# From group 6 on, one DMA transposes q and k of both groups of a block, and one DMA transposes x of both

## The chip, the cores and the metric

The kernel runs on one core of a Trainium2 chip. Its metric is the device time of one execution in microseconds (us). The engines carry the names of the profile: PE (TensorE, matmul), PEld (its weight load), DVE (VectorE), ACT (ScalarE), POOL (GpSimd) and SP (SyncE, which here only issues DMAs). All of SP's DMAs go into one queue, q1, and the stores that POOL issues go into q0.

## The reference

Attention inside chunks of 64 tokens, then a feed-forward layer with a squared ReLU. Cut to what matters:

```python
# q, k, v: (8 batches, 8 heads, 576 tokens, 64)
scores = scale * np.matmul(q_c, k_c.transpose(0, 1, 2, 4, 3))   # per chunk of 64 tokens
scores = scores - np.max(scores, axis=-1, keepdims=True)
attn = np.exp(scores)
attn = attn / (np.sum(attn, axis=-1, keepdims=True) + 1e-09)
out = np.matmul(attn, v_c)
x = out.transpose(0, 2, 1, 3).reshape(B * S, H * D)             # (4608, 512)
h = np.maximum(x @ w_in, 0.0)                                   # w_in (512, 2048)
return (h * h @ w_out).astype(np.float32)                       # w_out (2048, 512)
```

## The kernel before

**Tiling.** The 4608 tokens are cut into 18 groups of 256 tokens (four chunks), and two groups make a block of 512. There are nine blocks, j = 0 to 8. Block j holds groups 2j and 2j+1. Groups 14 and 15 are put together from the leftover chunks of four batches each, so their loads are more and smaller.

**Software pipeline.** While PE works on the feed-forward of block j, the attention of block j+1 (`nxt`) is worked between its matmuls, and the inputs of block j+2 (`far`) are loaded, cast and transposed. The order is written out by hand. A block is a row of slots: for j from 2 on, slots 0 to 15 are the 16 tiles of `ffn_in` (four matmuls of 128x512 each), and slots 16 to 29 are the 14 half products of `ffn_out` (eight matmuls of 128x256 each). In block 1, `ffn_in` is in two halves and has slots 0 to 31. After each slot the loop at L663 to L673 first issues one load, if the slot is among `go_slots`, and then the steps that the plan has there.

The steps that the change touches are these, in the order in which a group goes through them:

- `C`, `cast_qk` (L252): two casts, q and k from float32 to bfloat16, into the tile `qkb`. They run on POOL for groups under 8 and on ACT from group 8 on.
- `TD`, `transpose_qk_dma` (L263): one DMA transpose on SP from `qkb` to `qkT`, 128x2048 bfloat16 (512 KB) for a group. It is used from group 4 on.
- `SC`, `scores` (L271): 32 small matmuls from `qkT`, and the exponential on ACT into the tile `e`.
- `AV`, `values` (L303): matmuls of `e` with v, and the division on DVE into the tile `x` (L325).
- `XT`, `transpose_x` (L331): from group 6 on, one DMA transpose on SP from `x` to half of the block's `xT`, 128x1024 bfloat16 (256 KB) for a group. `ffn_in` of that block reads `xT` (L380).

SP[...] takes its instructions in program order: a transpose that waits for its source holds back every load that is written behind it. The plan for j from 3 on (L644):

```python
slots = {SC: (6, 6), AV: (9, 13), XT: (12, 16), C: (18, 22), TD: (20, 24)}
```

The pair of numbers is for the first and the second group. `SC` is at (8, 10) in block 2, at (8, 8) in block 3, at (7, 7) in block 4 and at (5, 5) where the next groups are whole. In block 1 the far groups 6 and 7 have `C` at 36 and 40 and `TD` at 42 and 45 (L635).

Between `C` and `TD` of the two groups lie ACT's other duties in `ffn_out`: the copies n1 (L492, after slot 17) and n2 (L501, after slot 21), which take a product out of PSUM before PE may add the next product of the same chain.

Of the kernel before, what the change touches and what calls it, by code (L numbers as in the profile page):

```python
# [11 lines left out]
BF16 = mybir.dt.bfloat16  # L12
# [5 lines left out]
def kernel(  # L18
# [9 lines left out]
    nc = tc.nc  # L28

    B, H, S, D = q.shape  # L30
# [4 lines left out]
    n_hp = H // 2  # L35
# [26 lines left out]
    att_pool = ctx.enter_context(tc.tile_pool(name="att", bufs=3))  # L62
# [123 lines left out]
    xTs = {}  # L186
# [4 lines left out]
    state = {}  # L191

    def transpose_paired(g, which, psb):

        src = qk[g][which].bitcast(BF16).rearrange(
            "p t h d -> p (t h d)").rearrange("p (h i d) -> p h i d", h=H, i=2)
        dst = psb.rearrange("c (h i q) -> c h i q", h=n_hp, i=2)
        for hp in range(n_hp):
            for i in range(2):
                for a in range(2):  # L200
                    nc.tensor.transpose(  # L201
                        out=dst[64 * a:64 * a + 64, hp, i, :],
                        in_=src[:, 2 * hp + a, i, 1::2],
                        identity=ident)
# [6 lines left out]

    def transpose_qk(g, q_pool, k_pool):
        if ("qkT", g) not in state:
            state["qkT", g] = att_pool.tile(
                [128, 2, 2, n_hp, 128], BF16, name="qkT", bufs=4)
        qkT = state["qkT", g]
        for which, pool in enumerate((q_pool, k_pool)):
            if pool is None:
                continue
            copy = nc.scalar.copy if which else nc.vector.tensor_copy  # L220
            if pool is ps_ffn:
                bank = pool.tile([128, 512], FP32, name="ps_ffn")
            else:
                bank = pool.tile([128, 1024], FP32, name="ps_att")
            bank = bank.bitcast(BF16)[:, 0:1024]
            transpose_paired(g, which, bank)
            copy_paired(copy, qkT[:, which], bank)
# [22 lines left out]
                rhs=ident[:, None, :].to_broadcast([128, m, 128]), start=True, stop=True)  # L250

    def cast_qk(g):  # L252
        qkb = att_pool.tile([128, 2, 2 * H * D], BF16, name="qkb", bufs=2)
        state["qkb", g] = qkb

        copy = nc.gpsimd.tensor_copy if g < 8 else nc.scalar.copy
        q_sb, k_sb = (x.rearrange("p t h d -> p (t h d)") for x in qk[g])
        copy(
            out=qkb[:, 0].rearrange("p (i h d) -> p i h d", i=2, h=H),
            in_=q_sb.rearrange("p (h i d) -> p i h d", h=H, i=2))  # L260
        copy(out=qkb[:, 1], in_=k_sb)  # L261

    def transpose_qk_dma(g):  # L263
        qkb = state.pop(("qkb", g))
        qkT = att_pool.tile([128, 2, 2, n_hp, 128], BF16, name="qkT", bufs=4)
        state["qkT", g] = qkT
        nc.sync.dma_start_transpose(
            out=qkT.rearrange("c w t h q -> c (w t h) q"),
            in_=qkb.rearrange("p w c -> p (w c)"))

    def scores(g):  # L271
        qkT = state.pop(("qkT", g))
        by_plane = g >= FIRST_DMA_T

        def queries(a, t, hp, p):
            x = qkT[64 * a:64 * a + 64, 0]
            if by_plane:
                p0 = (2 * t + p) * CH // 2
                return x[:, :, hp, p0:p0 + CH // 2]
            return x[:, t, hp, p * 64:p * 64 + 64]  # L280

        ps = ps_att.tile([128, 1024], FP32, name="ps_att")
        for hp in range(n_hp):
            for t in range(2):
                for a in range(2):
                    for p in range(2):
                        c = p ^ a
                        cols = slice(p * 64, p * 64 + 64)
                        o0 = a * 512 + hp * 128 + t * 64
                        nc.tensor.matmul(  # L290
                            out=ps[64 * c:64 * c + 64, o0:o0 + 64],
                            lhsT=qkT[64 * a:64 * a + 64, 1, t, hp, cols],
                            rhs=queries(a, t, hp, p),
                            start=True, stop=True)
        e = att_pool.tile([128, 2, n_hp, 2, 64], BF16, name="e")
        state["e", g] = e
        e_out, s_in = e.rearrange("p a h t q -> p (a h t q)"), ps
        if by_plane:
            e_out = e.rearrange("p a h t (q i) -> p (a h t) q i", i=2)
            s_in = ps.rearrange("p (b i q) -> p b q i", i=2, q=CH // 2)  # L300
        nc.scalar.activation(out=e_out, in_=s_in, func=AF.Exp, scale=scale)  # L301

    def values(g, tiles=(0, 1)):  # L303
        e = state["e", g]
        veb = v_even[g % NV].bitcast(BF16)
        vob = [v_odd[odd_tile[g, c] % NO].bitcast(BF16) for c in range(4)]
        if 0 in tiles:
            state["x", g] = att_pool.tile([128, 2, n_hp, 2, D], BF16, name="x", bufs=3)
        x = state["x", g]
        for t in tiles:  # L310
            ps = ps_att.tile([128, 2, 512], FP32, name="ps_att")
            for hp in range(n_hp):
                for a in range(2):
                    for p in range(2):
                        c = p ^ a
                        vb = vob[2 * t + p] if a else veb[:, t]
                        nc.tensor.matmul(  # L317
                            out=ps[64 * p:64 * p + 64, a, hp * (D + 1):(hp + 1) * (D + 1)],
                            lhsT=e[64 * c:64 * c + 64, a, hp, t, :],
                            rhs=vb[64 * c:64 * c + 64, hp, 1::2],  # L320
                            start=True, stop=True)
            o = ps[:, :, 0:n_hp * (D + 1)].rearrange("p a (h d) -> p a h d", d=D + 1)
            rec = att_pool.tile([128, 2, n_hp], FP32, name="rec", bufs=4)
            nc.vector.reciprocal(out=rec, in_=o[:, :, :, D])  # L324
            nc.vector.tensor_tensor(  # L325
                out=x[:, t].rearrange("p h a d -> p a h d"),
                in0=o[:, :, :, 0:D],
                in1=rec.to_broadcast([128, 2, n_hp, D]),
                op=ALU.mult)

    def transpose_x(g):  # L331
        j, c = place[g]
        if j not in xTs:
            xTs[j] = att_pool.tile([128, BT // 128, n_dt, 128], BF16, name="xT", bufs=2)
        x = state.pop(("x", g))
        dst = xTs[j][:, c // 128:c // 128 + 2].rearrange("p t h q -> p (t h) q")
        if g >= FIRST_DMA_X:
            nc.sync.dma_start_transpose(out=dst, in_=x.rearrange("p t h a d -> p (t h a d)"))
            return
        ps = ps_att.tile([128, 1024], FP32, name="ps_att")  # L340
        psb = ps.bitcast(BF16)[:, 0:1024].rearrange("p (b q) -> p b q", q=128)
        for t in range(2):
            for hp in range(n_hp):
                nc.tensor.transpose(
                    out=psb[:, t * n_hp + hp, :],
                    in_=x[:, t, hp].rearrange("p a d -> p (a d)"),
                    identity=ident)
        copy = nc.vector.tensor_copy if g == blocks[1][0] else nc.scalar.copy
        copy(out=dst, in_=psb)  # L349

    C, TD = cast_qk, transpose_qk_dma
    SC, AV, XT = scores, values, transpose_x

    def TA(g):
        transpose_qk(g, ps_att, ps_att)
# [254 lines left out]
    for j, grps in enumerate(blocks):  # L610
        nxt = blocks[j + 1] if j + 1 < len(blocks) else []
        far = blocks[j + 2] if j + 2 < len(blocks) else []
        plan = {}

        def at(slot, f, g):
            plan.setdefault(slot, []).append((f, g))
# [9 lines left out]
        elif j == 1:  # L626
# [7 lines left out]
                    at(slot, f, g)  # L634
            for i, g in enumerate(far):  # L635
                at(36 + 4 * i, C, g)
                at(42 + 3 * i, TD, g)
            at(2, sum_quarters(b11_p_b12, b11, b12), None)
            at(12, sum_quarters(b12_p_b22, b12, b22), None)
            at(20, sum_quarters(b21_p_b22, b21, b22), None)  # L640
            phases = [ffn_in(1, [(0, 256, FT_ORDER), (256, 256, FT_ORDER)]), ffn_out(1)]
        else:
            loads, go_slots = pieces(far), range(32)
            slots = {SC: (6, 6), AV: (9, 13), XT: (12, 16), C: (18, 22), TD: (20, 24)}  # L644
            if j == 3:
                slots.update({SC: (8, 8), AV: (10, 14), XT: (13, 17)})
                go_slots = [*range(6), *range(13, 32)]
# [3 lines left out]
                slots.update({SC: (5, 5), AV: (8, 12), XT: (11, 15)})  # L651
            if j == 2:
                loads = itertools.chain(*map(v_pieces, nxt), loads)
                slots = {SC: (8, 10), AV: (12, 15), XT: (15, 18), C: (20, 23), TD: (22, 25)}
                go_slots = [*range(16), 23, 24, *range(26, 36)]
            for f in (SC, AV, XT):
                for i, g in enumerate(nxt):
                    at(slots[f][i], f, g)
            for f in (C, TD):
                for i, g in enumerate(far):  # L660
                    at(slots[f][i], f, g)
            phases = [ffn_in(j, [(0, BT, FT_ORDER)]), ffn_out(j)]
        slot = 0  # L663
        for phase in phases:
# [40 lines left out]
```

## Time and profile before

| | us |
|---|---|
| median of 4 runs | 285.84 (283.2 to 290.56) |
| the profiled execution | 284.9 |
| its span on the core | 283.1 |
| around the span | 1.8 |
| PE at work at a clock of 1.00, blocks 2 to 6, each | 28.0 to 28.2 of 28.1 to 28.4 |

For each block from group 6 on, the transposes of q and k as the trace has them. An issue is the start of SP's instruction. A landing is that time plus the time to landing which the trace gives for it. "First scores" is the start of PE's score matmuls of the pair, which need these landings.

| groups | issued in block | first TD issued | second TD issued | first landed | second landed | first scores | second scores |
|---|---|---|---|---|---|---|---|
| 6, 7 | 1 | 79.4 | 84.2 | 86.3 | 92.1 | 90.90 | 93.11 |
| 8, 9 | 2 | 106.7 | 111.7 | 113.5 | 117.8 | 119.05 | 119.4 |
| 10, 11 | 3 | 136.2 | 140.7 | 142.8 | 146.4 | 146.30 | 146.7 |
| 12, 13 | 4 | 162.2 | 164.0 | 166.2 | 172.4 | 172.69 | 173.0 |
| 14, 15 | 5 | 189.1 | 194.1 | 194.7 | 200.8 | 201.63 | 202.0 |
| 16, 17 | 6 | 219.8 | 221.8 | 226.5 | 230.6 | 229.16 | 230.69 |

Where the scores of a pair run as one stretch of 64 matmuls in 0.71 us, the start of the second group is its middle. Such a table is read row by row: the column of the second landing against the two columns of the scores says how much time is left.

### The profile page before, as it was taken

The numbers are of one execution on the slowest core, as the hardware profiler recorded it, in microseconds if no ns is written. First come the engines' busy times: TensorE is split into PE (matmuls) and PEld (weight loads), VectorE is DVE, ScalarE is ACT, GpSimd is POOL, SyncE is SP. The second block draws the span as 40 slices with busy tenths as digits, with TensorE's granted clock in tenths as the row PEclk, the third lists the DMA queues.
The fourth block names the chain that finished last, engine by engine and source line by source line (L and its number), as shares of the span: only waits on it lengthen the run. The fifth ranks groups of instructions, "written<-read, shape, count | busy, mean of one in ns | idle before, by whom it ended". The sixth has DMA issues, their size and how long they took to land.

```text
span 283.1 us, 7169 instructions
## 1 busy us (share of the span) xinstructions
PE 270.1 (95%) x2954; PEld 175.4 (62%) x2954; DVE 185.8 (66%) x303; ACT 163.2 (58%) x277; POOL 55.7 (20%) x92
## 2 busy tenths in 40 slices
PE   1999999999999999999999999999999989999994
PEld 1554444778774487458745874587457734874583
DVE  1255514899943495579558953995399538955792
ACT  1458705786348862876287629762876286218710
POOL 2037843240161004000400040004000400060012
PEclk9999999999999999999999999999999999999999
DMA  7999999999998999998999899479799952142003
GB/s 201 242 325 362 360 340 237 299 218 219 202 238 239 226 212 211 280 251 167 241 256 221 180 258 252 100 160 213 209 244 185 191 150 39 37 105 46 1 28 123
DMA packets 140817, 57.10 MB, mean 202 GB/s; under 512 B 110640, under 2 KB 137520, under 8 KB 140784
## 3 DMA queue, kind: packets, MB, share of 16 engines
q1 hardware_dynamic: 137744, 47.33, 75.1%
q0 software_dynamic: 2896, 9.18, 9.6%
q8 instruction: 23, 0.38, 0.6%
q10 hardware_dynamic: 144, 0.13, 0.1%
q14 instruction: 10, 0.08, 0.1%
HBM read 36.70 MB, written 9.44 MB: 163 GB/s over the span
## 4 chain that ended last, share of the span: by engine, by line
PE 68%; DVE 15%; DMA 7%; ACT 5%; issue 3%; SPq 1%; ACTq 0%; DVEq 0%
PE ps_ffn L380 29%; PE ps_ffn L448 27%; DVE x L325 5%; DVE gT L395 5%; PE ps_ffn L538 5%; DMA k_sb<-in_k_dram 4%; DMA qkT<-qkb 3%; DVE w_st L408 3%; ACT rl L391 3%; PE ps_ffn L248 1%; ACT e L301 1%; PE ps_ffn L201 1%; PE ps_att L290 1%; DVE rec L324 1%; PE ps_att L317 1%
## 5 line engine op out<-in xcount | busy, mean ns | idle before, releaser
L380 PE MATMUL ps_ffn<-xT,w_in_bf 128*128 128x512 bf16 (+1 forms) x648 | 130.1, 356 | 0.2 <-DVE xT L349 0.2
L395 DVE TENSOR_TENSOR gT<-rl 128x512 bf16<-128x512 f32 (+2 forms) x130 | 74.0, 599 | 64.4 <-ACT rl L391 63.0
L391 ACT ACTIVATE rl<-ps_ffn 128x512 f32<-128x512 f32 (+2 forms) x162 | 86.0, 548 | 24.5 <-PE ps_ffn L380 21.9
L380 PEld LDWEIGHTS <-w_in_bf 128*128 128x128 bf16 x648 | 61.3, 98 | 56.6 <-DVE xT L349 0.4
L448 PEld LDWEIGHTS <-w_st 128*128 128x128 bf16 x640 | 61.7, 98 | 9.0 <-DVE w_st L408 1.8
L408 DVE TENSOR_TENSOR w_st<-gT 128x2048 bf16<-128x2048 bf16 x40 | 47.4, 1220 | 0.2
L448 PE MATMUL ps_ffn<-w_out_bf,w_st 128*128 128x256 bf16 x384 | 45.1, 273 | 0.4
L476 POOL DMA_DIRECT2D out_dram<-o_sb x25 | 17.8, 714 | 126.8 <-DVE o_sb L408 122.2
L448 PE MATMUL ps_ffn<-w_sum,w_st 128*128 128x256 bf16 x256 | 29.6, 273 | 0.0
L448 PEld LDWEIGHTS <-gT 128*128 128x128 bf16 x256 | 24.6, 98 | 5.0 <-DVE gT L395 0.8
L325 DVE TENSOR_TENSOR x<-ps_att,rec 128x512 bf16<-128x512 f32 x36 | 24.9, 692 | 1.2
L528 ACT COPY o_sb<-ps_ffn 128x512 f32<-128x512 f32 (+1 forms) x8 | 4.5, 560 | 35.4 <-PE ps_ffn L448 35.4
L301 ACT ACTIVATE e<-ps_att 128x1024 bf16<-128x1024 f32 x18 | 17.9, 1020 | 6.4 <-PE ps_att L290 6.4
L393 ACT ACTIVATE gT<-rl 128x512 bf16<-128x512 f32 (+2 forms) x32 | 18.4, 576 | 1.0
L448 PE MATMUL ps_ffn<-w_out_bf,gT 128*128 128x256 bf16 x128 | 15.6, 273 | 0.2 <-DVE gT L395 0.2
L448 PE MATMUL ps_ffn<-w_sum,gT 128*128 128x256 bf16 x128 | 15.3, 273 | 0.0
L538 PE MATMUL ps_ffn<-w_out_bf,gT 128*128 128x512 bf16 x64 | 14.5, 380 | 0.0
L169 POOL CAST w_in_bf<-w_st 128x512 bf16<-128x512 f32 (+2 forms) x12 | 9.9, 840 | 18.3 <-DMA w_st<-in_moe_w_in_dram 18.3
L501 ACT COPY n<-ps_ffn 128x512 f32<-128x512 f32 (+1 forms) x9 | 4.8, 538 | 12.3 <-PE ps_ffn L448 12.3
L317 PEld LDWEIGHTS <-e 64*64 64x64 bf16 x576 | 6.5, 107 | 7.4 <-issue 2.2
L261 ACT CAST qkb<-k_sb 128x1024 bf16<-128x1024 f32 x10 | 10.5, 1047 | 0.1
L290 PEld LDWEIGHTS <-qkT 64*64 64x64 bf16 x576 | 6.1, 110 | 7.2 <-issue 3.4
(53 smaller groups left out, 162.3 us busy)
## 6 DMA issues: line engine op xcount, KB each, us to landing
q_sb<-in_q_dram SPq DMA_DIRECT2D x16, 512.0 KB, 6.2
out_dram<-o_sb POOLq DMA_DIRECT2D x29, 256.0 KB, 4.6
k_sb<-in_k_dram SPq DMA_DIRECT2D x24, 256.0 KB, 5.9
ve_sb<-in_v_dram SPq DMA_DIRECT2D x32, 128.0 KB, 4.1
w_st<-in_moe_w_in_dram SPq DMA_DIRECT2D x8, 512.0 KB, 6.6
w_st<-in_moe_w_out_dram SPq DMA_DIRECT2D x8, 512.0 KB, 5.9
vo_sb<-in_v_dram SPq DMA_DIRECT2D x24, 128.0 KB, 3.7
k_sb<-in_k_dram SPq DMA_DIRECT2D x4, 512.0 KB, 7.1
```

The source lines that it names most:

```text
L169: copy(out=dst, in_=st[:, rows].rearrange("p a (f t) -> p a t f", t=2)[:, :, t])
L261: copy(out=qkb[:, 1], in_=k_sb)
L301: nc.scalar.activation(out=e_out, in_=s_in, func=AF.Exp, scale=scale)
L325: nc.vector.tensor_tensor(out=x[:, t].rearrange("p h a d -> p a h d"), in0=o[:, :, :, 0:D], in1=rec.to_broadcast([128, 2, n_hp, D]), op=AL ...
L380: nc.tensor.matmul(out=h[:, 0:n], lhsT=w_in_bf[:, dt, ft * 128:(ft + 1) * 128], rhs=xT[:, c // 128:(c + n) // 128, dt, :], start=(dt == 0) ...
L391: nc.scalar.activation(out=rl[:, 0:n], in_=h[:, 0:n], func=AF.Relu)
L393: nc.scalar.activation(out=gT[:, ft, c:c + n], in_=rl[:, 0:n], func=AF.Square)
L395: nc.vector.tensor_tensor(out=gT[:, ft, c:c + n], in0=rl[:, 0:n], in1=rl[:, 0:n], op=ALU.mult)
L408: engine.tensor_tensor(out=out, in0=in0, in1=in1, op=op)
L448: nc.tensor.matmul(out=outs[t], lhsT=a[:, i, t * 128:(t + 1) * 128], rhs=b[:, i, :], start=(first and i == 0 and (last or t == 0)), stop=( ...
L476: dma.dma_start(out=out[t0:t0 + HT, col:col + HD].rearrange("(t p) d -> p t d", p=128), in_=o_sb.rearrange("p (t d) -> p t d", d=HD))
L538: nc.tensor.matmul(out=o_ps[tt], lhsT=gT[:, ft, tt * 128:(tt + 1) * 128], rhs=w_out_bf[:, ft, :], start=(ft == 0), stop=(ft == n_ft - 1))
```

## The change

It has five parts.

1. `qkb` becomes one tile for both groups of a block with one buffer (before: one group, two buffers). `qkT` becomes a tile for both groups with two buffers (before: one group, four buffers). The bytes are the same.
2. From group 6 on the two `TD` become one, `TDB`, 1 MB, at slot 44 of block 1 (before 42 and 45), slot 24 of block 2 (before 22 and 25) and slot 22 of the later blocks (before 20 and 24).
3. `C` of the second group goes from slot 22 to 20 (in block 2 from 23 to 22).
4. `x` becomes a tile for both groups with two buffers (before: one group, three buffers), and `XT` issues nothing for the first group and one transpose of 512 KB for both at the second group's slot.
5. `e` has two buffers in place of three.

```diff
     def cast_qk(g):
-        qkb = att_pool.tile([128, 2, 2 * H * D], BF16, name="qkb", bufs=2)
-        state["qkb", g] = qkb
+        if g % 2 == 0:
+            state["qkb", g // 2] = att_pool.tile(
+                [128, 2, 2, 2 * H * D], BF16, name="qkb", bufs=1)
+        qkb = state["qkb", g // 2][:, g % 2]
...
+    def qkT_of(g):
+        if g % 2 == 0:
+            state["qkT", "block", g // 2] = att_pool.tile(
+                [128, 2, 2, 2, n_hp, 128], BF16, name="qkT", bufs=2)
+        return state["qkT", "block", g // 2][:, g % 2]
...
+    def transpose_qk_dma_block(g):
+
+        for i in range(2):
+            state["qkT", g + i] = qkT_of(g + i)
+        nc.sync.dma_start_transpose(
+            out=state["qkT", "block", g // 2].rearrange("c g w t h q -> c (g w t h) q"),
+            in_=state["qkb", g // 2].rearrange("p g w c -> p (g w c)"))
...
-        e = att_pool.tile([128, 2, n_hp, 2, 64], BF16, name="e")
+        e = att_pool.tile([128, 2, n_hp, 2, 64], BF16, name="e", bufs=2)
...
-            state["x", g] = att_pool.tile([128, 2, n_hp, 2, D], BF16, name="x", bufs=3)
+            if g % 2 == 0:
+                state["x", "block", g // 2] = att_pool.tile(
+                    [128, 2, 2, n_hp, 2, D], BF16, name="x", bufs=2)
+            state["x", g] = state["x", "block", g // 2][:, g % 2]
...
         if g >= FIRST_DMA_X:
-            nc.sync.dma_start_transpose(out=dst, in_=x.rearrange("p t h a d -> p (t h a d)"))
+
+            if g % 2:
+                nc.sync.dma_start_transpose(
+                    out=xTs[j].rearrange("p t h q -> p (t h) q"),
+                    in_=state["x", "block", g // 2].rearrange("p g t h a d -> p (g t h a d)"))
             return
...
                 at(36 + 4 * i, C, g)
-                at(42 + 3 * i, TD, g)
+            at(44, TDB, far[0])
...
-            slots = {SC: (6, 6), AV: (9, 13), XT: (12, 16), C: (18, 22), TD: (20, 24)}
+            slots = {SC: (6, 6), AV: (9, 13), XT: (12, 16), C: (18, 20), TD: 22}
...
-                slots = {SC: (8, 10), AV: (12, 15), XT: (15, 18), C: (20, 23), TD: (22, 25)}
+                slots = {SC: (8, 10), AV: (12, 15), XT: (15, 18), C: (20, 22), TD: 24}
```

More of the change, by code (lines that the diff above doesn't have):

```diff
@@ L213, in transpose_qk @@
         if ("qkT", g) not in state:
-            state["qkT", g] = att_pool.tile(
-                [128, 2, 2, n_hp, 128], BF16, name="qkT", bufs=4)
+            state["qkT", g] = qkT_of(g)
         qkT = state["qkT", g]
@@ L261, in cast_qk @@
         copy(out=qkb[:, 1], in_=k_sb)
+    def qkT_of(g):
[3 more added lines that the diff above has]
+        return state["qkT", "block", g // 2][:, g % 2]
     def transpose_qk_dma(g):
-        qkb = state.pop(("qkb", g))
-        qkT = att_pool.tile([128, 2, 2, n_hp, 128], BF16, name="qkT", bufs=4)
-        state["qkT", g] = qkT
+        state["qkT", g] = qkT = qkT_of(g)
         nc.sync.dma_start_transpose(
             out=qkT.rearrange("c w t h q -> c (w t h) q"),
-            in_=qkb.rearrange("p w c -> p (w c)"))
+            in_=state["qkb", g // 2][:, g % 2].rearrange("p w c -> p (w c)"))
+    def transpose_qk_dma_block(g):
[4 more added lines that the diff above has]
+            in_=state["qkb", g // 2].rearrange("p g w c -> p (g w c)"))
     def scores(g):
@@ L349, in transpose_x @@
         copy(out=dst, in_=psb)
-    C, TD = cast_qk, transpose_qk_dma
+    C, TD, TDB = cast_qk, transpose_qk_dma, transpose_qk_dma_block
     SC, AV, XT = scores, values, transpose_x
@@ L658 @@
                     at(slots[f][i], f, g)
-            for f in (C, TD):
-                for i, g in enumerate(far):
-                    at(slots[f][i], f, g)
+            for i, g in enumerate(far):
+                at(slots[C][i], C, g)
+            if far:
+                at(slots[TD], TDB, far[0])
             phases = [ffn_in(j, [(0, BT, FT_ORDER)]), ffn_out(j)]
```

## The prediction

> **What bounds the kernel now.** I read the page's busy times first, then the stretches from block 2 on.
>
> ```profile
> PE 270.1 (95%) x2954; PEld 175.4 (62%) x2954; DVE 185.8 (66%) x303; ACT 163.2 (58%) x277; POOL 55.7 (20%) x92
> ...
> q1 hardware_dynamic: 137744, 47.33, 75.1%
> q0 software_dynamic: 2896, 9.18, 9.6%
> ```
> ```profile
> 195.50:223.90 28.40, 28.14 (x307) 18.13 (x305) 20.44 (x31) 18.18 (x28) 2.87 (x5) 1.00 1.00 212
> 223.90:253.00 29.10, 28.02 (x307) 18.27 (x305) 20.44 (x31) 14.63 (x24) 3.68 (x7) 1.00 0.39 87
> ...
> sum 196.20, PE 194.52 PEld 126.01 DVE 137.60 ACT 119.03 POOL 25.14; mean PE 27.79 PEld 18.00 DVE 19.66 ACT 17.00 POOL 3.59
> ```
>
> In each row the second number is PE's busy time. Over blocks 2 to 8 PE is idle for 196.20 - 194.52 = 1.7 us, at a clock of 1.00. So PE bounds, and whatever frees SP or the DMA queue can win 1.7 us at most. The DMA share is about 1.0 beside PE: the second resource is nearly full, so a transfer can be late. The next question is where PE waits, which PE's timeline shows at the scores of groups 16 and 17, and where it nearly waits:
>
> ```profile
> 229.16 0.45 PE L290 MATMUL ps_att<-qkT 64*64 64x64 bf16 x32
> 230.69 0.44 PE L290 MATMUL ps_att<-qkT 64*64 64x64 bf16 x32 [1.08 <-DMA qkT<-qkb]
> ```
> ```profile
> 90.90 0.45 PE L290 MATMUL ps_att<-qkT 64*64 64x64 bf16 x32
> 91.28 1.90 PE L380 MATMUL ps_ffn<-xT,w_in_bf 128*128 128x512 bf16 x8
> 93.11 0.45 PE L290 MATMUL ps_att<-qkT 64*64 64x64 bf16 x32
> ```
>
> The one long stall, 1.08 us, is a second TD that landed at 230.6. In the other rows of the table above, the second landing is 0.2 to 1.3 us ahead of the second scores. So scores follow landings closely everywhere, and the change will be felt through one number: when the joint transpose lands, against the **first** scores of the pair.
>
> [...] SP waited 13.9 us for DVE's x in front of L338, 9.8 us at the longest, and nothing behind it was issued meanwhile. [...]
>
> **What a transpose costs.** The rows of the tiles qkb and x, SP's side and landing:
>
> ```profile
> L267 SPq DMA_TRANSPOSE qkT<-qkb x14: 1697/3222/5253, 59.7 to 221.8; - x14
> ...
> DMA to landing us min/median/max: 4.0/6.7/8.8
> ```
> ```profile
> L338 SPq DMA_TRANSPOSE xT<-x x12: 1232/1274/2469, 103.9 to 241.1; - x12
> ...
> DMA to landing us min/median/max: 3.1/3.4/5.4
> ```
>
> At best 256 KB land in 3.1 us and 512 KB in 4.0, so 256 KB more cost 0.9. For 1 MB that is 4.0 + 2 x 0.9 = 5.8 us, **the low end**. In traffic, the second TD of each pair took 7.9, 6.1, 5.7, 8.4, 6.7 and 8.8 us (table), a mean of 7.3; with 1.8 for the other 512 KB this makes **9.1, which I take**. **The high end** is that nothing is shared: 2 x 6.7 = 13.4.
>
> **The change part by part.**
>
> *TDB in place of two TD.* It can be issued when the second casts are done and SP has got through what is written before it. For groups 6 and 7 the casts end it, on POOL, whose second k waits for its load:
>
> ```profile
> 81.73 1.04 POOL L258 CAST qkb<-q_sb 128x1024 bf16<-128x1024 f32 x1 [1.66 <-DMA q_sb<-in_q_dram]
> 83.18 1.04 POOL L261 CAST qkb<-k_sb 128x1024 bf16<-128x1024 f32 x1 [0.41 <-DMA k_sb<-in_k_dram]
> ```
>
> Issue at 83.18 + 1.04 = 84.2, landing at 84.2 + 9.1 = 93.3. The first scores stood at 90.90: PE waits **2.4 us**, because the 512 KB that landed at 86.3 before now go behind the same cast. Low end: 90.0, no wait; high end: 97.6, 6.7 us.
>
> The other issues, at the latest: (8,9) XT at 103.9 plus 1.7 plus two loads of 0.6 is 106.8, and the casts end at 106.9; (10,11) 137.0, when SP had reached the first TD (136.2) plus the one load between the two; (12,13) 162.2, where SP was at the first TD, now ahead of two XT issues in one; (14,15) 189.1 plus half of the loads between the TDs, 191.3; (16,17) 219.9. Plus 9.1: 116.0, 146.1, 171.3, 200.4, 229.0. First scores: 119.05, 146.30, 172.69, 201.63, 229.16. All are in time, by 0.2 at the tightest, and at (16,17) the stall of **1.1 us goes**. What is late next there is the landing itself, with 0.2 us to spare.
>
> Queued behind TDB on SP: in block 1 the v loads of groups 6 and 7 (issued from 87.3 on, landing in about 4 us, wanted by AV at 95.3 and 98.4). Up to 1.8 us more transposing ahead of them is covered if AV is itself 2.4 late; if not, up to 1 us. I take 0. In later blocks the next loads are wanted a block later.
>
> *The second C two slots earlier.* ACT had a hole between the casts, and the copy n2 (L501) now comes after both:
>
> ```profile
> 214.43 1.05 ACT L261 CAST qkb<-k_sb 128x1024 bf16<-128x1024 f32 x1
> 217.10 0.59 ACT L501 COPY n<-ps_ffn 128x512 f32<-128x512 f32 x1 [1.62 <-PE ps_ffn L448]
> 217.58 1.05 ACT L258 CAST qkb<-q_sb 128x1024 bf16<-128x1024 f32 x1
> ```
>
> A cast follows a cast after 0.95 us, so four end at about 213.5 + 4 x 0.96 = 217.3; n2 goes from 217.1 to 217.3 and ends at 217.9. PE's next product of that chain begins at 218.65. In blocks 3 to 5 the same sum gives n2 from 133.0, 161.1 and 189.2, done 0.5 us ahead of PE at 134.06, 162.18 and 190.26. Cost 0. A second k that came late would cost PE its lateness less 0.5; both loads landed before these times (the last at 186.7 in block 5, cast at 188.3).
>
> *One XT for both.* x of the second group is done at 101.3, 128.6, 156.8, 183.6, 212.6 and 241.1; the next `ffn_in` begins at 111.2, 139.3, 167.4, 195.5, 223.9 and 253.0. As much data as a TD, so 4.0 to 8.8 us. The tightest is the first: issued at 103.9, where SP had the first XT, it lands at 107.9 to 112.7; the two transposes of before, 105.3 the later, landed by 110.7. I take 0, up to 1.5 against. SP's wait for the first x (4 us in block 5 and 9.8 in block 7) disappears, but only loads for a block later stood behind it: gain 0.
>
> *Buffers.* qkb with one buffer: the next block's first cast waits for TDB's landing, nearest 93.3 against 101.3. For groups 6 and 7 the cast at 76.0 would wait at worst for group 5's TD (issued 66.1, at most 8.8 us: 74.9). e with two: its reader two groups back is some 20 us earlier. x and qkT: two blocks deep as before. Cost 0, hidden by a block's work.
>
> **Sum.** +2.4 - 1.1 = +1.3 us. The profiled execution had 284.9, so 286.2; it stood 0.9 below the median of 285.84, so the median goes to 287.1. I say 287.0.
>
> **The rivals.**
>
> *A, TDB lands quickly and only the stall goes.* At 84.2 the queue is nearly empty; up to 6.7 us of landing, groups 6 and 7 don't wait. Against it: the second TD, issued at the same moment, took 7.9 alone. Time: 285.84 - 1.1 = 284.7, at the very best 1.7 less, 284.1.
>
> *B, slower: the landing doubles.* Place: all six pairs' first scores. Late by 13.4 from the issues above: 6.7 + 1.3 + 4.1 + 2.9 + 3.1 + 4.1 - 1.1 = 21.1 us, 307. For it: from the first issue to the second landing a pair took 10.2 to 12.7 us. Against: that includes SP's waits and loads between, and the bytes are the same. It decides from where the sum passes 5.7 us (2%): at 10.7 us of landing, (6,7) 4.0, (10,11) and (16,17) 1.4 each, (14,15) 0.4, (12,13) 0.2, less 1.1, is 6.3. So 1.6 us above my value is enough.
>
> *C, the change doesn't do what it says:* one instruction of 1 MB is carried out as two transposes with a landing each, or groups 6 and 7 are hidden by another wait. Then nothing but the last stall moves: 285 to 286.
>
> **How the numbers follow.** Forecast 0.55, A 0.21, B 0.19, C 0.05. About 2%, or 5.7 us, is what a measurement of this kernel can tell from no change. Forecast, A and C lie within it; only a spread of runs as in before (283.2 to 290.6) could make A faster by 2%, so 0.02. Slower is B, 0.19, and the rest is same. The range begins under A's best, at 283.6, and reaches into B, to 292.0, which leaves out most of B and little of A.
>
> **What would show it.** Right: six TDBs with landings of 7 to 10 us; a PE wait of 1 to 3 us before the scores of group 6 near 91, released by the DMA qkT<-qkb; none before 229; PE busy all through blocks 3 to 6; L501 0.2 to 0.5 us later, with no wait behind it. Wrong: waits at L290 in most blocks (B), none near 91 (A), twelve TDs still (C), or a wait at L448 for L501 or at L380 for xT, which I priced at 0.

## The result and the profile after

| | before | after |
|---|---|---|
| median of the runs, us | 286.79 (17 runs, 283.2 to 294.27) | 290.2 (12 runs, 286.62 to 295.84) |
| the profiled execution, us | 284.9 | 290.41 |
| its span, us | 283.1 | 288.6 |

The ratio is 1.014, 95% interval 1.0095 to 1.0186: slower, by less than 2%. Executions of one program spread over up to 13 us here and a ratio takes only those within 1.5% of each kernel's fastest, so a difference of one per cent needs more than one draw.

The spans differ by 5.5 us. In the stretches from one block's `ffn_in` to the next block's (block 2, 3, 4 and 7 of the changed kernel: length, then the busy time of PE, PEld, DVE, ACT and POOL with counts, PE clock, DMA share, GB/s) they are easily found:

```profile
82.40:116.40 34.00, 29.92 (x307) 18.72 (x306) 17.31 (x31) 18.38 (x28) 5.14 (x7) 0.95 0.93 185
116.40:144.50 28.10, 28.00 (x307) 18.11 (x305) 20.52 (x31) 18.05 (x28) 2.83 (x5) 1.00 1.17 234
144.50:173.30 28.80, 28.07 (x306) 18.09 (x304) 20.62 (x31) 18.18 (x28) 2.83 (x5) 1.00 1.08 232
...
229.80:258.50 28.70, 28.00 (x307) 18.20 (x305) 20.44 (x31) 14.62 (x24) 3.66 (x7) 1.00 0.37 88
...
sum 202.30, PE 196.33 PEld 126.53 DVE 137.73 ACT 118.96 POOL 25.14; mean PE 28.05 PEld 18.08 DVE 19.68 ACT 16.99 POOL 3.59
```

The same stretch of the kernel before, its block 2:

```profile
83.00:111.20 28.20, 28.20 (x307) 18.24 (x306) 17.30 (x31) 18.27 (x28) 5.12 (x7) 1.00 0.97 210
```

Block 2 is the one that stands out: 34.0 us where the kernel before needed 28.2. PE is idle there for 34.00 - 29.92 = 4.1 us, **and** its busy time is 29.9 where 28.2 did the same 307 matmuls before: its clock was 0.95, not 1.00. Blocks 4 and 7 have 0.7 us of idle time each; block 7 had 1.1 before. Block 1 (not in the rows) became 0.5 us shorter. So 4.1 + 1.7 + 0.6 - 0.4 - 0.5 = 5.5 us.

What PE waited for is in its list of waits (us in total, times, longest) and in its timeline around block 2's scores (start, duration, count, and in brackets the idle time before and its releaser). The scores of L290 stand at L303 in the changed kernel, and `ffn_in` of L380 at L400:

```profile
PE ps_att L303 <- DMA qkT<-qkb: 5.4, 3, 4.1
```
```profile
94.47 0.58 PE L303 MATMUL ps_att<-qkT 64*64 64x64 bf16 x32 [4.08 <-DMA qkT<-qkb]
94.98 3.38 PE L400 MATMUL ps_ffn<-xT,w_in_bf 128*128 128x512 bf16 x8
98.29 0.45 PE L303 MATMUL ps_att<-qkT 64*64 64x64 bf16 x32
```

The scores of group 6 wait for the joint transpose. The second row answers to the row at 91.28 of before: the same eight matmuls took 1.90 us there and 3.38 here. Finer stretches show why:

```profile
82.40:90.40 8.00, 7.99 (x38) 3.47 (x36) 2.13 (x5) 6.28 (x11) 3.13 (x4) 1.00 0.83 172
90.40:94.50 4.10, 0.03 (x4) 0.03 (x5) 0.85 (x2) 0.62 (x2) 0.00 (x0) 1.00 0.95 214
94.50:97.50 3.00, 3.00 (x38) 1.30 (x39) 0.00 (x0) 1.56 (x2) 0.00 (x0) 0.52 0.95 212
97.50:101.00 3.50, 3.50 (x76) 1.64 (x75) 0.85 (x2) 2.63 (x6) 0.00 (x0) 0.93 1.01 242
```

Behind the idle stretch PE runs at half clock, for 3.41 us by the trace's clock records: half of 3.41 is the 1.7 us of additional busy time.

POOL's timeline and SP's, and SP's side of the tile qkb, show where the lateness starts (SP's rows: start, duration of the issue, count):

```profile
81.31 1.04 POOL L259 CAST qkb<-q_sb 128x1024 bf16<-128x1024 f32 x1 [1.38 <-DMA q_sb<-in_q_dram]
82.89 1.04 POOL L262 CAST qkb<-k_sb 128x1024 bf16<-128x1024 f32 x1 [0.53 <-DMA k_sb<-in_k_dram]
```
```profile
75.50 3.71 SPq L119 DMA_DIRECT2D k_sb<-in_k_dram  x2
83.95 6.17 SPq L280 DMA_TRANSPOSE qkT<-qkb  x1
90.18 1.13 SPq L147 DMA_DIRECT2D ve_sb<-in_v_dram  x2
```
```profile
L280 SPq DMA_TRANSPOSE qkT<-qkb x6: 4201/5770/7427, 84.0 to 225.7; - x6
...
DMA to landing us min/median/max: 4.2/9.3/11.8
```

SP stands still from 79.2 to 83.95. In the kernel before it began to issue group 6's transpose at 79.4 in this gap, while k of group 7 was still being loaded. Now that transpose waits for group 7's last cast, which ended at 82.89 + 1.04 = 83.93, and half of the work starts 4.5 us later.

| groups | TDB issued | landed after, us | first scores | idle before them |
|---|---|---|---|---|
| 6, 7 | 83.95 | about 10.5 | 94.47 | 4.08 |
| 8, 9 | 112.08 | 9.3 | 124.23 | 0 |
| 10, 11 | 140.38 | 11.8 | 152.18 | 0.63 |
| 12, 13 | 167.48 | 6.8 | 178.58 | 0 |
| 14, 15 | 196.65 | 9.9 | 207.51 | 0 |
| 16, 17 | 225.72 | 10.0 | 235.8 | 0.69 |

(The first landing is read from the scores that it released. For this pair it took 10.1 to 10.7 us in the six traces that have the joint transpose of it.)

### The profile page after: what moved, and what is told of

It reads as the page before. It is cut to its first block, busy times and chain, and to the rows that moved or that the text cites. A ratio compares the mean times of both kernels' runs of the same rounds, so it can differ in the third digit from the quotient of the medians.

```text
span 288.6 us, 7144 instructions
## 1 busy us (share of the span) xinstructions
PE 271.9 (94%) x2954; PEld 176.0 (61%) x2954; DVE 186.6 (65%) x303; ACT 162.8 (56%) x277; POOL 55.3 (19%) x92
## 4 chain that ended last, share of the span: by engine, by line
PE 64%; DMA 15%; DVE 11%; ACT 5%; issue 2%; SPq 0%; POOL 0%; ACTq 0%
PE ps_ffn L400 28%; PE ps_ffn L468 25%; DMA qkT<-qkb 11%; PE ps_ffn L558 5%; DVE gT L415 5%; DMA k_sb<-in_k_dram 4%; DVE x L341 4%; ACT rl L411 3%; DVE w_st L428 2%; PE ps_att L303 2%; ACT e L314 2%; PE ps_ffn L247 1%; PE ps_att L333 1%; PE ps_ffn L201 1%; DVE rec L340 1%
## 5 line engine op out<-in xcount | busy, mean ns | idle before, releaser
L400 PE MATMUL ps_ffn<-xT,w_in_bf 128*128 128x512 bf16 (+1 forms) x648 | 131.7, 358 | 0.2 <-DVE xT L369 0.2
L400 PEld LDWEIGHTS <-w_in_bf 128*128 128x128 bf16 x648 | 61.7, 98 | 57.7 <-issue 1.6
L468 PEld LDWEIGHTS <-w_st 128*128 128x128 bf16 x640 | 61.7, 98 | 9.1 <-DVE w_st L428 2.0
L428 DVE TENSOR_TENSOR w_st<-gT 128x2048 bf16<-128x2048 bf16 x40 | 47.4, 1220 | 0.2
L468 PE MATMUL ps_ffn<-w_out_bf,w_st 128*128 128x256 bf16 x384 | 45.1, 273 | 0.4
L468 PE MATMUL ps_ffn<-w_sum,w_st 128*128 128x256 bf16 x256 | 29.6, 273 | 0.0
L468 PEld LDWEIGHTS <-gT 128*128 128x128 bf16 x256 | 24.6, 98 | 5.1 <-DVE gT L415 0.7
L468 PE MATMUL ps_ffn<-w_out_bf,gT 128*128 128x256 bf16 x128 | 15.6, 273 | 0.1
L468 PE MATMUL ps_ffn<-w_sum,gT 128*128 128x256 bf16 x128 | 15.3, 273 | 0.0
L303 PEld LDWEIGHTS <-qkT 64*64 64x64 bf16 x576 | 6.2, 111 | 11.8 <-DMA qkT<-qkb 6.9
L303 PE MATMUL ps_att<-qkT 64*64 64x64 bf16 x576 | 7.9, 199 | 5.7 <-DMA qkT<-qkb 5.4
L333 PEld LDWEIGHTS <-e 64*64 64x64 bf16 x576 | 6.5, 107 | 7.4 <-issue 2.2
L259 ACT CAST qkb<-q_sb 128x1024 bf16<-128x1024 f32 x10 | 10.5, 1047 | 0.0
```

The source lines that it names most:

```text
L259: copy(out=qkb[:, 0].rearrange("p (i h d) -> p i h d", i=2, h=H), in_=q_sb.rearrange("p (h i d) -> p i h d", h=H, i=2))
L303: nc.tensor.matmul(out=ps[64 * c:64 * c + 64, o0:o0 + 64], lhsT=qkT[64 * a:64 * a + 64, 1, t, hp, cols], rhs=queries(a, t, hp, p), start=T ...
L400: nc.tensor.matmul(out=h[:, 0:n], lhsT=w_in_bf[:, dt, ft * 128:(ft + 1) * 128], rhs=xT[:, c // 128:(c + n) // 128, dt, :], start=(dt == 0) ...
L428: engine.tensor_tensor(out=out, in0=in0, in1=in1, op=op)
L468: nc.tensor.matmul(out=outs[t], lhsT=a[:, i, t * 128:(t + 1) * 128], rhs=b[:, i, :], start=(first and i == 0 and (last or t == 0)), stop=( ...
```

## The experiments

My theory was that the loss comes from groups 6 and 7 alone, from the late issue and from the half clock behind the idle stretch. The rivals were a cost of the 1 MB instruction itself, of the joint transpose of x or of the earlier casts, and a wait that moves on when one is removed. All edits are to the changed kernel. Medians are of the kernel and of the kernel before on the same chips.

**1. Groups 6 and 7 transposed singly again; all else joint** (split67), and the same program a second time (split67_again).

```diff
-            at(44, TDB, far[0])
+            for i, g in enumerate(far):
+                at(42 + 3 * i, TD, g)
```

> The changed kernel, but groups 6 and 7 keep their two transposes at slots 42 and 45. Theory (the joint transpose of groups 6 and 7 waits for the second cast, lands after the first scores, and PE's idle time there also costs clock): the idle time near 90 us (4.1 us) and the low clock behind it (about 1.6 us) both go, the granted clock returns to 0.998, and the time is 0.99 to 1.005 of before. Rival (joint transposes are late in all blocks, groups 6 and 7 being only the most visible): the time stays at 1.01 or more, with idle time at the scores of later blocks.

> The same program as split67 (two transposes for groups 6 and 7, all else of the change kept), timed in more rounds and profiled again. Theory (the change without the joint transpose of groups 6 and 7 is a little faster than before, since the landings of the later blocks have more room): 0.990 to 0.998 of before, a profile with less than 1 us of idle time at the scores from block 2 on and a clock of 1.00. Rival (the 0.6% of the first time was the draw of executions): an interval around 1.00.

Measured: 288.03 against 288.45, ratio 0.994 (0.9899 to 0.9981) in 20 runs; the second time 290.12 against 287.59, ratio 1.0155 (1.0086 to 1.0224) in 6 runs. These intervals exclude each other. A gain of 0.6% is thus not established, nor a loss of 1.5%, and what I expected of the repeat (0.990 to 0.998, less than 1 us of idle time at the scores) didn't come; over both, the mean of the 26 runs is 288.8 against 288.4 for all 167 runs of the kernel before in this study. What both traces agree on is block 2. The stretches of blocks 2 and 3 of split67:

```profile
82.40:110.60 28.20, 28.20 (x307) 18.25 (x306) 17.30 (x31) 18.17 (x28) 4.83 (x8) 1.00 1.03 223
110.60:138.70 28.10, 28.00 (x307) 18.07 (x305) 20.52 (x31) 18.05 (x28) 2.83 (x5) 1.00 1.06 231
```

Idle time and half clock are gone from block 2, by one edit of slots. But both profiled executions (288.0 and 289.0 us, where the program's fastest took 283.7) wait later, at the scores of groups 10 and 11: 2.1 us in the first, and in split67_again as its timeline shows:

```profile
119.64 0.71 PE L303 MATMUL ps_att<-qkT 64*64 64x64 bf16 x64 [0.79 <-DMA qkT<-qkb]
149.84 0.98 PE L303 MATMUL ps_att<-qkT 64*64 64x64 bf16 x64 [2.87 <-DMA qkT<-qkb]
```

So the joint transposes of other pairs stand on the edge as well, and whether one of them falls over it differs from one execution to the next.

**2. Both transposes singly, written behind both casts** (back2back), then in reverse order (reversed67). The first was to keep the late issue and undo the merging alone.

```diff
-            at(44, TDB, far[0])
+            for g in far:
+                at(45, TD, g)
```
```diff
-            at(44, TDB, far[0])
+            for g in reversed(far):
+                at(44, TD, g)
```

> The changed kernel, but groups 6 and 7 have two transposes, both at slot 45, so that the second follows the first at once and neither is issued before the second cast unless the queue is early. Theory (half of the loss is the late issue, half that the first scores wait for the whole megabyte): the first lands 6.5 to 7.5 us after the issue, at 90.5 to 91.5, the second at 93.5 to 94.5, PE is idle 0 to 1.5 us in all, the clock stays at 1.0, and the time is 0.995 to 1.005 of before. Rival (one instruction of 1 MB is itself slower than two of 512 KB): both land by 92, and PE is hardly idle.

> The changed kernel, but groups 6 and 7 have two transposes of 512 KB one after the other, group 7's first, so that both stand behind the second cast, as the joint one does, and the first scores wait for the second of them. Theory (the loss is the issue behind the second cast and the wait for all of the megabyte, not the size of the instruction): the second lands 9.5 to 11 us after the first is issued, idle time of 3 to 4.5 us near 90, 1.010 to 1.018 of before. Rival (one instruction of 1 MB is slower than two of 512 KB): the second lands within 8 us, idle time below 1.5 us, below 1.005.

back2back measured 288.23, ratio 0.9964 (0.9924 to 1.0004), but it didn't do what was meant. SP was ahead of the program's other engines, and the first transpose didn't wait for group 7's casts: it was issued at 80.61, the second at 84.85. It is split67 once more. In reversed67 the first one needs the last cast, so that both are late in fact. It measured 289.45, ratio 1.0139 (1.0022 to 1.0257). SP's timeline, and PE's:

```profile
83.69 7.25 SPq L272 DMA_TRANSPOSE qkT<-qkb  x2
```
```profile
92.93 0.64 PE L303 MATMUL ps_att<-qkT 64*64 64x64 bf16 x32 [2.77 <-DMA qkT<-qkb]
93.51 3.21 PE L400 MATMUL ps_ffn<-xT,w_in_bf 128*128 128x512 bf16 x8
```

Two transposes of 512 KB, issued from the same moment as the one of 1 MB, release group 6 after 92.93 - 83.69 = 9.2 us against 10.5 (10.1 to 10.7 in six traces). PE is idle for 2.8 us in place of 4.1, both a little under what I expected, and the half clock is there (0.50 from 92.90 to 96.00). So the form of the instruction is worth some 0.9 to 1.5 us of this wait, by this one trace; the rest is the late issue and the whole megabyte ahead of the first scores. These two stand together in every run that has the loss, so how they share it isn't shown.

**3. Only groups 6 and 7 joint, all else as before** (join67_only), and the same program again (join67_again). Tiles and buffers are those of the changed kernel; its core:

```diff
-            slots = {SC: (6, 6), AV: (9, 13), XT: (12, 16), C: (18, 20), TD: 22}
+            slots = {SC: (6, 6), AV: (9, 13), XT: (12, 16), C: (18, 22), TD: (20, 24)}
...
-            if g % 2:
-                nc.sync.dma_start_transpose(
-                    out=xTs[j].rearrange("p t h q -> p (t h) q"),
-                    in_=state["x", "block", g // 2].rearrange("p g t h a d -> p (g t h a d)"))
+            nc.sync.dma_start_transpose(out=dst, in_=x.rearrange("p t h a d -> p (t h a d)"))
```

> The tiles and buffers of the changed kernel, but only groups 6 and 7 share one transpose of q and k; from group 8 on the transposes of q and k, their casts, and all transposes of x stand as in the kernel before. Theory (the loss is that one joint transpose): idle time of 3 to 4.5 us before the scores of group 6 near 90 us, half clock for some 3 us behind it, and 1.012 to 1.022 of before. Rival (the loss needs the other joint transposes too): below 1.008.

> The same program as join67_only (only groups 6 and 7 joined, all later transposes as before), timed in more rounds and profiled again, because its 3.5% rest on four executions and are more than the loss at groups 6 and 7 explains. Theory (the idle time near 90 us with its half clock costs 1.5 to 2%, and what came on top was late landings of groups 15 and 17 in that draw): 1.013 to 1.025 of before, the idle time near 90 again 3 to 4.5 us. Rival (the shift by this idle time makes the separate transposes of the later blocks late every time): 1.028 or more, with idle time of 1.5 us or more at the scores of groups 15 or 17 again.

Measured: 296.1 against 288.52, ratio 1.0352 (1.0213 to 1.0492) in 4 runs, and 290.69 against 289.72, ratio 1.0122 (1.0056 to 1.0189) in 6. The one joint transpose is enough for the loss in block 2: 4.06 and 3.26 us of idle time before 94.42 and 93.64, each with half clock behind it (0.50 from 94.40 to 100.00 in the first draw; the second draw's execution had a mean clock of 0.988). The rest of the 3.5% are later waits, at second transposes that stand as in the kernel before (groups 15 and 17). The first draw's timeline shows two long ones:

```profile
209.60 0.45 PE L303 MATMUL ps_att<-qkT 64*64 64x64 bf16 x32 [1.46 <-DMA qkT<-qkb]
...
240.18 0.65 PE L303 MATMUL ps_att<-qkT 64*64 64x64 bf16 x32 [2.97 <-DMA qkT<-qkb]
```

The second draw has the last of them again, with 1.83 us and half clock (0.50 from 237.46 on), where the kernel before had 1.08; so the rival of join67_again, that the shift makes later transposes late, holds in part, though its time doesn't. Why the two draws lie so far apart stays open.

**4. The other parts.** x_joint_only keeps the tiles and the joint transpose of x and takes casts and transposes of q and k back to the plan of before; qk_joint_late does the opposite, with the joint q,k of the later blocks and split67's edit.

```diff
-            at(44, TDB, far[0])
+            for i, g in enumerate(far):
+                at(42 + 3 * i, TD, g)
...
-            slots = {SC: (6, 6), AV: (9, 13), XT: (12, 16), C: (18, 20), TD: 22}
+            slots = {SC: (6, 6), AV: (9, 13), XT: (12, 16), C: (18, 22), TD: (20, 24)}
```
```diff
-            if g % 2:
-                nc.sync.dma_start_transpose(
-                    out=xTs[j].rearrange("p t h q -> p (t h) q"),
-                    in_=state["x", "block", g // 2].rearrange("p g t h a d -> p (g t h a d)"))
+            nc.sync.dma_start_transpose(out=dst, in_=x.rearrange("p t h a d -> p (t h a d)"))
```

> The changed kernel with one transpose of x for both groups and all the new tiles and buffers, but the transposes of q and k and the casts as before. Theory (what is left of the change without groups 6 and 7 gains a little because fewer scores wait for a landing, which is the work of the joint transposes of q and k): this one is without effect, 0.996 to 1.004 of before. Rival (the gain of 0.6% without the joint transpose of groups 6 and 7 comes from SP not waiting for the first x): 0.990 to 0.996.

> As split67, but x is transposed for each group alone again, at its own slot. Theory (the joint transposes of q and k from group 8 on, with the earlier second cast, are what gains; the joint transpose of x is without effect): 0.990 to 0.999 of before. Rival (the gain needs both, since two transposes of x keep SP longer from the joint transpose behind them): 0.999 to 1.008.

Measured: 287.65, ratio 1.0028 (0.9979 to 1.0077), and 287.73, ratio 1.0057 (1.0021 to 1.0094); the means of their 20 runs are 288.3 and 287.7, against 288.4. The second ratio lies in the range of its rival, not of its theory. Neither part moves the time by as much as the draws differ. In x_joint_only's timeline one `ffn_in` waited for xT:

```profile
202.66 0.45 PE L303 MATMUL ps_att<-qkT 64*64 64x64 bf16 x32 [0.65 <-DMA qkT<-qkb]
225.31 5.34 PE L400 MATMUL ps_ffn<-xT,w_in_bf 128*128 128x512 bf16 x24 [1.07 <-DMA xT<-x]
231.83 0.45 PE L303 MATMUL ps_att<-qkT 64*64 64x64 bf16 x32 [0.81 <-DMA qkT<-qkb]
```

That is within the 1.5 us which the prediction held against this part; the trace of the changed kernel itself has no such wait.

**5. Scores of 6 and 7 later, joint transpose kept** (sc10, sc12, later67): if the lateness is all, later scores should hide it. Block 2's slots:

```diff
-                slots = {SC: (8, 10), AV: (12, 15), XT: (15, 18), C: (20, 22), TD: 24}
+                slots = {SC: (10, 10), AV: (12, 15), XT: (15, 18), C: (20, 22), TD: 24}
```
```diff
-                slots = {SC: (8, 10), AV: (12, 15), XT: (15, 18), C: (20, 22), TD: 24}
+                slots = {SC: (12, 12), AV: (14, 15), XT: (15, 18), C: (20, 22), TD: 24}
```
```diff
-                slots = {SC: (8, 10), AV: (12, 15), XT: (15, 18), C: (20, 22), TD: 24}
+                slots = {SC: (14, 14), AV: (17, 19), XT: (19, 21), C: (20, 22), TD: 24}
```

> The changed kernel, but the scores of group 6 stand at slot 10 of block 2 in place of 8. Two slots are 1.74 us of other matmuls. Theory (an idle stretch of about 4 us halves the clock for about 3 us[...]): the idle time falls from 4.1 to about 2.3 us and the clock stays at 1.0, so the time falls by 1.7 + 1.6 = 3.3 us against the changed kernel, to 1.00 to 1.005 of before. Rival (the clock falls after any idle time in the scores): it falls by 1.7 us alone, and the clock in the 3 us behind the scores is near 0.5 again.

> The changed kernel with its joint transpose of groups 6 and 7, but their scores at slot 12 of block 2 and the values at 14 and 15, all still inside the first matrix product. Theory (idle time at these scores plus 1.7 us[...]): four slots are 3.5 us, so the idle time falls from 4.1 to between 0 and 1.7 us, no half clock, and the time is 0.992 to 1.004 of before. Rival (the idle time moves to the values, which stand close behind, and to block 4): 1.005 or more, with idle time at L333 or at the scores of groups 10 and 11.

> The changed kernel, but in block 2 the scores of groups 6 and 7 stand at slot 14, the values at 17 and 19, and the transposes of x at 21. Theory (nothing but the landing against the first scores costs): no idle time at the scores, xT lands before the next block, and the time is 0.985 to 1.00 of before. Rival (what is moved later meets the next block): idle time at L400 at the start of block 3, 1 us or more, and a time of 1.005 or more.

Measured: 289.65, ratio 1.0081 (1.003 to 1.0132); 290.88, ratio 1.0112 (1.001 to 1.0215) in 4 runs; 291.43, ratio 1.0095 (1.0048 to 1.0142). None wins the time back. In sc10 PE is idle for 3.1 us, where I had expected about 2.3, and the half clock comes all the same, behind less idle time than the 4.08 us of the changed kernel. Its stretches:

```profile
92.30:95.40 3.10, 0.05 (x1) 0.00 (x0) 0.76 (x2) 0.60 (x1) 0.00 (x0) 0.92 1.16 274
95.40:97.40 2.00, 1.95 (x67) 1.34 (x68) 0.00 (x0) 1.26 (x2) 0.00 (x0) 0.50 1.36 212
```

In sc12 1.5 us remain at the scores, without half clock (1.00 from 96.00 to 99.00), but its rival came true: PE waits 1.4 us at the values (L333), and 3.35 us with half clock at the scores of groups 10 and 11 (0.55 from 155.00 to 157.00 and 0.60 from there to 159.00). In later67 none remain at the scores; there the wait moves on to the values, whose divisions stand on DVE behind the work of L428. DVE's timeline of later67, and PE's:

```profile
100.47 2.36 DVE L428 TENSOR_TENSOR w_st<-gT 128x2048 bf16<-128x2048 bf16 x2
102.75 0.20 DVE L340 RECIPROCAL rec<-ps_att 128x8 f32<-128x8 f32 x1
102.98 0.69 DVE L341 TENSOR_TENSOR x<-ps_att,rec 128x512 bf16<-128x512 f32 x1
```
```profile
103.73 0.22 PE L333 MATMUL ps_att<-ve_sb,e 64*64 64x65 bf16 x2 [1.17 <-DVE x L341]
104.57 0.22 PE L333 MATMUL ps_att<-ve_sb,e 64*64 64x65 bf16 x2 [0.51 <-DVE x L341]
```

These two are 1.7 us, and 2.4 us at the scores of 10 and 11 follow. Moving the scores later thus trades one wait for another: at the later slots the values meet other work of DVE. This accounts for the one profiled execution; it isn't shown for the mean of the 20 runs.

**6. The next wait given one slot more** (split67_sc8): split67, with block 4's scores later.

```diff
-                slots.update({SC: (7, 7), AV: (10, 14), XT: (13, 17)})
+                slots.update({SC: (8, 8), AV: (10, 14), XT: (13, 17)})
```

> Two transposes for groups 6 and 7 at slots 42 and 45, and the scores of groups 10 and 11 one slot later, at slot 8 of block 4. Theory (0.87 us more before these scores takes off idle time there, where the joint transpose took 10 to 12.7 us to land in the traces so far): the lower of both versions, 0.988 to 0.996 of before. Rival (these scores wait in disturbed executions only): as without the later slot, 0.990 to 0.998.

Measured: 288.18, ratio 1.001 (0.9957 to 1.0064): no gain. Its profiled execution waited 2.98 us for groups 8 and 9 and 3.15 for 10 and 11: landings vary by more than a slot of 0.87 us (6.8 to 11.8 us in the changed kernel's trace).

**All runs together.** Single ratios of about one per cent contradicted each other, so I also took the mean over every run, against the mean of the 167 runs of the kernel before (288.4). The six programs in which group 6 stands behind both casts (the changed kernel, sc10, sc12, later67, reversed67, join67 in both draws) had means of 290.6 to 293.0 each; their 70 runs together have 291.2, ratio 1.010 (95% interval by resampling the runs, 1.007 to 1.013). The five in which group 6 is transposed on its own when its cast is done (split67 in both draws, back2back, x_joint_only, qk_joint_late, split67_sc8) had 287.7 to 288.8; their 106 runs have 288.3, ratio 1.000 (0.997 to 1.002). No program of one side lies within the other's range, and the fastest run of each says the same: 285.6 to 289.3 us on the first side, 283.6 to 285.2 on the second. The intervals take runs as independent, which the two draws of split67 and of join67 speak against; by single draws the two sides come close (290.3 for split67_again, 290.6 for the lowest of the others). This is the result that I trust: the loss hangs on that one ordering, and the rest of the change, taken together, neither wins nor loses anything that can be measured (the tiles for two groups and the two buffers of `e` stand in all these programs and weren't undone on their own). No version clearly beat the kernel before.

## Why the prediction was right, and where its sizes were off

- **The place and the releaser held.** The wait is at the scores of group 6 near 91, behind the DMA qkT<-qkb; the issue was put at 84.2 and came at 83.95. Split67 shows that this step makes the wait, and reversed67 that the late issue and the whole megabyte together make most of it.
- **The landing, taken as 9.1 us, was 10.5** there, so that the wait was 4.1 us and not 2.4. The mean over all six (9.3, 11.8, 6.8, 9.9, 10.0 and this one) is 9.7: a good mean, but a mean hides that each pair has its own margin. Fifteen of the 16 counts of this transpose's completion stand at 93.0 to 93.1 in the trace and the last at 94.43. The first scores started at 94.47, right behind it, so the last count alone held back PE for 1.3 us. That they wait for the whole transpose was my assumption in the prediction; no trace of before shows it, this one does. The late count isn't all that made this pair late, though: the scores were due at 94.47 - 4.08 = 90.39, and up to 93.10, where the other counts stand, they would still have waited for 2.7 us (an estimate from these figures). And in the kernel before, the second transpose of the pair had a late count too (the others up to 90.42, the last at 92.14).
- **A term was missing: the half clock.** It lasted 3.41 us behind the 4.1 of idle time and cost 1.7 us. The prediction had no such term: in the trace of before the clock stands at 1.00 from 12.23 to 281.88. A wait of 2.4 us, as the prediction had it, could have brought it too: 2.38 us did in later67 and 2.14 in split67, while 1.51 in sc12 didn't.
- **The stall at groups 16 and 17 went only in part**, from 1.1 to 0.7 us, as the landing took 10.0 and not 9.1; the 0.2 us to spare in the prediction were nothing against the spread of landings (6.8 to 11.8 us). For the same reason 10 and 11, which had 0.2 us as well, waited for 0.6.
- **What was costed at nothing cost nothing in the trace.** On ACT four casts run in a row (134.35 to 138.24 in block 3) and n2 follows at once, with no wait of PE at L468 for it. `ffn_in` at L400 waited for no xT. No wait for a buffer appeared.
- **The sum.** Predicted +1.3 us; the profiled execution's span has +5.5, the medians +3.4, the means over all runs 290.7 - 288.4 = +2.3. The step that was mis-sized is the first, "+2.4", measured 4.1 + 1.7 = 5.8 in one execution; the second, "- 1.1", was - 0.4. The measured median of 290.2 lay in the range, but the range is 8.4 us wide and would have held no change as well, so this says little. What the traces confirm is the place and the path. One reading was off: by the table the second landings stand 0.3 to 1.6 us ahead of the second scores, not 0.2 to 1.3; no sum uses it.
- **The rivals.** A needed a landing under 6.7 us: groups 12 and 13 alone came near it. B needed 10.7 in general: only 10 and 11 passed it. C is refuted by six transposes with one landing each. B's idea was nearer to the truth than its price: a landing 1.4 us above my value is what happened at the tightest pair.

Open: why executions of one program differ by up to 4%. In the traces it is the landings that differ (groups 10 and 11 kept PE waiting for 2.14 us in split67 and for 2.87 in the same program's second trace), but what makes one of them late wasn't tried. The clock of every run is on record and says more than one trace can: of the 150 runs of the kernel before that were taken beside the experiments, 84 had a mean clock of 0.994 or less (3.41 us at half clock, as in the changed kernel's trace, take 0.006), and these took 290.1 us on average, the others 286.6. The profiled execution of before had a clock of 0.998, so the prediction's 1.7 us as the most that can be won holds for that execution and not for the average. Of the changed kernel's 12 runs 11 had such a clock; of all 70 runs with group 6 behind both casts 55, of the 106 without 49. (The mean also counts the end of the kernel: the 0.998 of the profiled execution of before comes from there, where the clock was 0.50 from 281.88 to the end of the span at 283.1.)

## What to carry to other kernels

The merged transfer didn't start before its last source was there (83.95, after a cast that ended at 83.93), and its first reader waited for its last count (94.47, after 94.43): look at what the queue and the engines did between the two sources before merging (here a gap of 4.5 us that one transfer had filled), and take the margin of each reader against the longest landing (11.8 us here), not the mean (9.7). Price a wait of PE with the half clock that can follow it: here it followed 12 of the 14 waits of 1.83 to 4.08 us at the scores, and the changed kernel's 3.41 us of it cost 1.7 us. Where programs differ by a per cent, repeat one of them before believing an order.

## What the runs showed of the hardware that I had not expected

- **The half clock followed most of PE's longer waits, but the length of a wait alone doesn't decide.** The clock fell to 0.50 at idle stretches before scores of 4.08 us (the changed kernel), 4.06 and 2.97 (join67_only), 3.85 (back2back), 3.35 (sc12), 3.26 and 1.83 (join67_again), 3.10 (sc10), 2.87 (split67_again), 2.77 (reversed67), 2.38 (later67) and 2.14 (split67); but not at the 2.98 and 3.15 us of split67_sc8, nor at any of 1.51 us or less. In the changed kernel it lasted 3.41 us. It lasted longer in two traces: the clock was 0.50 in every stretch from 94.40 to 100.00 in join67_only (4.06 us of idle time) and from 150.60 to 156.00 in back2back (3.85 us). In the rows below, PE's busy time is the second number and the clock stands after POOL: the changed kernel and join67_again, each with the 3.41 us before the fall and the 3.41 behind it, then stretches of split67_sc8.

```profile
91.18:94.60 3.42, 0.13 (x16) 0.13 (x20) 0.30 (x1) 0.00 (x0) 0.00 (x0) 1.00 0.89 216
94.60:98.01 3.41, 3.41 (x40) 1.36 (x36) 0.42 (x1) 1.62 (x2) 0.00 (x0) 0.50 0.93 204
```
```profile
234.05:237.46 3.41, 1.58 (x69) 0.92 (x68) 1.58 (x3) 1.94 (x4) 0.00 (x0) 1.00 0.70 159
237.46:240.87 3.41, 3.41 (x10) 1.17 (x9) 0.06 (x1) 2.50 (x4) 0.00 (x0) 0.50 0.00 0
```
```profile
116.80:120.21 3.41, 1.65 (x8) 0.56 (x6) 1.77 (x3) 2.25 (x4) 0.00 (x0) 1.00 1.14 260
120.22:123.63 3.41, 2.20 (x72) 1.30 (x72) 0.00 (x0) 1.69 (x2) 0.00 (x0) 1.00 1.24 223
150.94:154.35 3.41, 1.58 (x69) 1.07 (x70) 0.06 (x1) 1.08 (x2) 0.00 (x0) 1.00 1.18 310
```

In the 3.41 us before the fall PE was busy for 0.13 us in the changed kernel and for 1.58 in join67_again; in split67_sc8 a stretch of the same length also had 1.58 us of work, and the clock stood at 1.00 in it and on to 160.00. What decides between these cases isn't shown. In join67_again PE was back at work at 236.60 and the clock fell at 237.46, so the half clock can fall on work that no longer waits for anything.

- **One transpose of 1 MB took 6.8 to 11.8 us to land** in one execution. For groups 6 and 7 it took 10.1 to 10.7 in six traces, where two of 512 KB from the same moment released the first reader in 9.2 (reversed67).
